# A fused multiply-add stream: y in two 64 KB loads, stores released by a semaphore after the third product

## The chip, the core and the metric

The kernel runs on one core of one Trainium2 chip. The metric is the device time of one execution in microseconds (us). Five runs of the kernel before are shown, and one further execution was taken with the hardware profiler. Sizes of "32 KB" and "64 KB" are bytes per partition; on 128 partitions they make transfers of 4 MB and 8 MB.

## The reference

```python
B, S, D = 1024, 16, 512      # bf16
def reference(x, y, gamma):  # x, y: [B, S, D], gamma: [D]
    return x + gamma * y
```

x, y and the result have 16,384 rows of 512 bf16 values, 16.78 MB each. So the kernel has to read 33.55 MB and write 16.78 MB, and for each element it does one product and one sum.

## The kernel before

Partition p holds the rows 128 p to 128 p + 127 of the flattened arrays, so each partition's part lies together in HBM. These 128 rows are cut into four pieces of 32 rows (`PIECES`), 32 KB per partition each. y has an SBUF buffer for all 128 rows and the results are written over it. x has a buffer of 64 rows, so that pieces 2 and 3 of x take the places of pieces 0 and 1.

**Queues.** SyncE (SP) issues all loads, in the order of the list `SP`, by `ring` (line 75 on): x 0, y 0, x 1, y 1, y 2, x 2, y 3, x 3, each of 4 MB (lines 88 and 91). ScalarE (ACT) issues gamma's load (line 85) and the four stores (line 95), by the list `ACT`. The two queues appear in the profile as q1 (SP) and q10 (ACT). The first x, the first y and gamma are moved to the head of the program (`EARLY`).

**Waits in the queues.** An engine executes its list in order, so a wait holds up everything behind it. A load of x that overwrites an old piece waits on the semaphore `s_add` for the add that has used the old piece: x 2 for add 0, x 3 for add 1 (`X_AFTER`). A store carries in its last number the add it waits for: stores 0, 1 and 2 all wait for add 2, store 3 for add 3.

**VectorE (DVE).** gamma is first spread over the 128 partitions: TensorE multiplies a row of ones with it into PSUM, and VectorE copies the result to SBUF (lines 104 to 110). Then, for each piece in turn, VectorE waits for the piece of y, multiplies it by gamma in place (line 115, "product"), waits for the piece of x and for the product, and adds (line 120, "add"). All eight instructions cover 128 x 16,384 elements.

**The end.** SP waits for the four adds and for all stores.

The lines that decide the order:

```python
X_AT = [0, 32, 0, 32]
X_AFTER = [-1, -1, 0, 1]
SP = [('x', 0), ('y', 0), ('x', 1), ('y', 1), ('y', 2), ('x', 2), ('y', 3), ('x', 3)]
ACT = [('g',), ('s', 0, 0, 2), ('s', 1, 1, 2), ('s', 2, 2, 2), ('s', 3, 3, 3)]
```

Of the kernel before, what the change touches and what calls it, by code (L numbers as in the profile page):

```python
# [3 lines left out]


PIECES = [32, 32, 32, 32]

X_AT = [0, 32, 0, 32]
X_AFTER = [-1, -1, 0, 1]


SP = [('x', 0), ('y', 0), ('x', 1), ('y', 1), ('y', 2), ('x', 2), ('y', 3), ('x', 3)]
ACT = [('g',), ('s', 0, 0, 2), ('s', 1, 1, 2), ('s', 2, 2, 2), ('s', 3, 3, 3)]

EARLY = [('x', 0), ('y', 0), ('g',)]
MULT, ADD = mybir.AluOpType.mult, mybir.AluOpType.add


def _take(sem, n, eng):


    return eng.wait_ge(sem, n).then_inc(sem, -n)  # L22


def kernel(
    tc: tile.TileContext,
    x: bass.AP,
    y: bass.AP,
    gamma: bass.AP,
    out: bass.AP,  # L30
):

    nc = tc.nc
    P = nc.NUM_PARTITIONS
    tc.close()
    tc.compile()  # L38

    xf = x.flatten_outer_dims()  # L40
    yf = y.flatten_outer_dims()
    of = out.flatten_outer_dims()
    N, D = xf.shape
    rows = N // P
    n = len(PIECES)
    assert sum(PIECES) == rows
    starts = [sum(PIECES[:c]) for c in range(n + 1)]
    dt = xf.dtype
    xv = xf.rearrange("(p n) d -> p n d", p=P)
    yv = yf.rearrange("(p n) d -> p n d", p=P)  # L50
    ov = of.rearrange("(p n) d -> p n d", p=P)

    gamma_row = nc.alloc_sbuf_tensor("gamma_row", [1, D], dt).ap()
    ones_row = nc.alloc_sbuf_tensor("ones_row", [1, P], dt).ap()
    gamma_sb = nc.alloc_sbuf_tensor("gamma_sb", [P, D], dt).ap()
    y_sb = nc.alloc_sbuf_tensor("y_sb", [P, rows, D], dt).ap()
    x_rows = max(a + r for a, r in zip(X_AT, PIECES))
    x_sb = nc.alloc_sbuf_tensor("x_sb", [P, x_rows, D], dt).ap()
    gamma_ps = nc.alloc_psum_tensor("gamma_ps", [P, D], mybir.dt.float32).ap()

    sem = nc.alloc_semaphore
    s_gamma, s_ones, s_ps, s_dve = sem("s_gamma"), sem("s_ones"), sem("s_ps"), sem("s_dve")
    s_x = [sem(f"s_x{c}") for c in range(n)]
    s_y = [sem(f"s_y{c}") for c in range(n)]
    s_add, s_end, s_out = sem("s_add"), sem("s_end"), sem("s_out")

    def piece(a, b=None):
        return slice(starts[a], starts[(a if b is None else b) + 1])

    def x_tile(c):  # L70
        return x_sb[:, X_AT[c] : X_AT[c] + PIECES[c], :]

    early, stores = [], 0

    def ring(eng, what, known=-1):

        nonlocal stores
        for w in what:
            kind, args = w[0], w[1:]
            need = X_AFTER[args[0]] if kind == "x" else args[2] if kind == "s" else -1  # L80
            if need > known:
                eng.wait_ge(s_add, need + 1)
                known = need
            if kind == "g":
                i = eng.dma_start(out=gamma_row, in_=gamma.unsqueeze(0)).then_inc(s_gamma, 16)
            elif kind == "x":
                c = args[0]
                i = eng.dma_start(out=x_tile(c), in_=xv[:, piece(c), :]).then_inc(s_x[c], 16)
            elif kind == "y":
                c = args[0]  # L90
                i = eng.dma_start(out=y_sb[:, piece(c), :], in_=yv[:, piece(c), :])
                i.then_inc(s_y[c], 16)
            else:
                r = piece(args[0], args[1])
                i = eng.dma_start(out=ov[:, r, :], in_=y_sb[:, r, :]).then_inc(s_out, 16)
                stores += 1
            if w in EARLY:
                early.append(i.ins)

    ring(nc.sync, SP)  # L100
    ring(nc.scalar, ACT)


    nc.vector.memset(ones_row, 1.0).then_inc(s_ones, 1)  # L104
    _take(s_ones, 1, nc.tensor)
    _take(s_gamma, 16, nc.tensor)
    nc.tensor.matmul(gamma_ps, ones_row, gamma_row, start=True, stop=True).then_inc(s_ps, 1)  # L107
    _take(s_ps, 1, nc.vector)
    nc.vector.tensor_copy(out=gamma_sb, in_=gamma_ps).then_inc(s_dve, 1)  # L109
    _take(s_dve, 1, nc.vector)  # L110

    for c in range(n):
        yt = y_sb[:, piece(c), :]
        _take(s_y[c], 16, nc.vector)
        nc.vector.tensor_tensor(  # L115
            out=yt, in0=yt, in1=gamma_sb[:, None, :].to_broadcast([P, PIECES[c], D]), op=MULT
        ).then_inc(s_dve, 1)
        _take(s_x[c], 16, nc.vector)
        _take(s_dve, 1, nc.vector)
        nc.vector.tensor_tensor(out=yt, in0=x_tile(c), in1=yt, op=ADD).then_inc(s_add, 1)  # L120


    nc.scalar.sem_inc(s_end, 1)
    _take(s_end, 1, nc.sync)
    _take(s_add, n, nc.sync)
    _take(s_out, 16 * stores, nc.sync)

    main = nc.main_func.blocks[0].instructions
    names = {i.name for i in early}
    for b in nc.main_func.blocks[1:]:  # L130
        for i in [i for i in b.instructions if i.name in names]:
            b.instructions.remove(i)
    for k, i in enumerate(early):
        main.insert(1 + k, i)


# [1 line left out]
_INS = ['x', 'y', 'gamma']  # L138
_OUTS = [((1024, 16, 512), 'bfloat16')]


# [23 lines left out]
```

## Time and profile before

| what | value |
|---|---|
| median of five runs | 120.96 us (120.2 to 121.08) |
| profiled execution, its own time | 120.48 us |
| its span, first to last instruction | 119.1 us |
| VectorE: four products | 34.8 us, 8689 ns each |
| VectorE: four adds | 34.8 us, 8692 ns each |
| VectorE idle before products | 17.6 us, of it 15.7 before the first |
| issue to landing, median: x / y / stores | 21.3 / 34.7 / 24.2 us |

The profile numbers the time from the first instruction. "Busy" of a compute engine is the time in which it executes; issuing a DMA isn't counted. The DMA rows give, for each queue, the number of packets, the megabytes and the share of sixteen DMA engines' span that these packets took. The time to landing of a transfer runs from its issue to its last completion, and so includes the time in which it stands behind earlier transfers of its queue.

### The profile page before, as it was taken

What the parts mean: (1) busy time and instruction counts of PE and PEld (TensorE: products, weight loads), DVE (VectorE), ACT (ScalarE), POOL (GpSimd) and SP (SyncE); (2) the same over time, 40 slices, a digit from 0 to 9 for tenths busy, and PEclk for the clock granted to TensorE, in tenths of its full rate; (3) what the DMA queues carried; (4) which work ended last, traced back from release to release, by engine and by line L of the source; (5) the groups of instructions that cost most, each with busy time, mean ns of one, the idle gap of its engine ahead of it and who ended that gap; (6) DMA issues with size and microseconds to landing.
All of it is one profiled execution on the core that took longest, in us unless ns stands there. A gap on an engine that the chain in (4) does not pass through costs nothing. (4 is left out here: it accounts for less than half of the span.)

```text
span 119.1 us, 84 instructions
## 1 busy us (share of the span) xinstructions
PE 0.6 (0%) x1; PEld 0.1 (0%) x1; DVE 70.2 (59%) x10; POOL 0.2 (0%) x4
## 2 busy tenths in 40 slices
PE   0100000000000000000000000000000000000000
PEld 0000000000000000000000000000000000000000
DVE  0100000699999399999999999999999400000000
POOL 0000000000000000000000000000000000000000
DMA  8989898989898998989898989989999898989895
GB/s 275 429 374 506 352 528 352 517 363 517 363 506 374 407 473 374 506 352 528 352 517 363 495 385 440 440 352 429 451 396 484 363 517 352 528 352 495 385 473 231
DMA packets 1730, 50.33 MB, mean 422 GB/s; under 512 B 193, under 2 KB 194, under 8 KB 194
## 3 DMA queue, kind: packets, MB, share of 16 engines
q1 hardware_dynamic: 1152, 33.55, 66.2%
q10 hardware_dynamic: 578, 16.78, 32.6%
HBM read 33.56 MB, written 16.78 MB: 422 GB/s over the span
## 5 line engine op out<-in xcount | busy, mean ns | idle before, releaser
L115 DVE TENSOR_TENSOR y_sb<-y_sb,gamma_sb 128x16384 bf16<-128x16384 bf16 x4 | 34.8, 8689 | 17.6 <-DVEq L22 17.6
L120 DVE TENSOR_TENSOR y_sb<-x_sb,y_sb 128x16384 bf16<-128x16384 bf16 x4 | 34.8, 8692 | 0.6
L109 DVE CAST gamma_sb<-gamma_ps 128x512 bf16<-128x512 f32 x1 | 0.7, 692 | 3.4 <-DVEq L22 3.4
L104 DVE MEMSET ones_row<- 1x128 bf16 x1 | 0.2, 165 | 2.0 <-PEq L38 2.0
L107 PE MATMUL gamma_ps<-gamma_row,ones_row 1*128 1x512 bf16 x1 | 0.6, 581 | 4.8 <-PEq L22 4.8
L107 PEld LDWEIGHTS gamma_ps<-gamma_row,ones_row 1*128 1x128 bf16 x1 | 0.1, 100 | 4.7 <-issue 4.7
L149 POOL MEMSET const-bfloat16-1.0<- 128x1 bf16 x1 | 0.1, 101 | 0.0
L149 POOL MEMSET const-uint8-127<- 128x1 uint8 x1 | 0.1, 101 | 0.0
L149 POOL MEMSET const-float32-0.0<- 128x1 f32 x1 | 0.1, 98 | 0.2 <-issue 0.2
L149 POOL MEMSET const-float32-1.0<- 128x1 f32 x1 | 0.1, 98 | 0.0
## 6 DMA issues: line engine op xcount, KB each, us to landing
x_sb<-in_x_dram SPq DMA_DIRECT2D x4, 4096.0 KB, 21.3
y_sb<-in_y_dram SPq DMA_DIRECT2D x4, 4096.0 KB, 34.7
out_dram<-y_sb ACTq DMA_DIRECT2D x4, 4096.0 KB, 24.2
gamma_row<-in_gamma_dram ACTq DMA_DIRECT2D x1, 1.0 KB
```

Of the source, the lines that this page charges most:

```text
L104: nc.vector.memset(ones_row, 1.0).then_inc(s_ones, 1)
L107: nc.tensor.matmul(gamma_ps, ones_row, gamma_row, start=True, stop=True).then_inc(s_ps, 1)
L109: nc.vector.tensor_copy(out=gamma_sb, in_=gamma_ps).then_inc(s_dve, 1)
L115: nc.vector.tensor_tensor(out=yt, in0=yt, in1=gamma_sb[:, None, :].to_broadcast([P, PIECES[c], D]), op=MULT).then_inc(s_dve, 1)
L120: nc.vector.tensor_tensor(out=yt, in0=x_tile(c), in1=yt, op=ADD).then_inc(s_add, 1)
L149: nc = _bacc.Bacc("TRN2", target_bir_lowering=False, num_devices=1)
```

## The change

The lists now name ranges of rows in place of numbers of pieces. The loads of x and the eight VectorE instructions stay in pieces of 32 rows; y is loaded in two transfers of 64 rows; the result is stored as 64, 32 and 32 rows. The order of the loads on SP is x 0-32, y 0-64, x 32-64, y 64-128, x 64-96, x 96-128. The last two wait for add 0 and add 1, as before. VectorE waits once for each load, at its first use.

A new semaphore `s_go` is increased by VectorE between product 2 and add 2, once product 2 is done. ACT waits for it ahead of its first store, and then for the adds of the rows that the store holds: add 1 for the first store, add 2 for the second, add 3 for the third. x 0-32, y 0-64 and gamma are at the head of the program.

```diff
-X_AT = [0, 32, 0, 32]
-X_AFTER = [-1, -1, 0, 1]
-SP = [('x', 0), ('y', 0), ('x', 1), ('y', 1), ('y', 2), ('x', 2), ('y', 3), ('x', 3)]
-ACT = [('g',), ('s', 0, 0, 2), ('s', 1, 1, 2), ('s', 2, 2, 2), ('s', 3, 3, 3)]
-EARLY = [('x', 0), ('y', 0), ('g',)]
+SP = [('x', 0, 32, 0), ('y', 0, 64), ('x', 32, 64, 32), ('y', 64, 128), ('x', 64, 96, 0), ('x', 96, 128, 32)]
+ACT = [('g',), ('s', 0, 64), ('s', 64, 96), ('s', 96, 128)]
+EARLY = (2, 1)
+DVE = [('m', 0), ('a', 0), ('m', 1), ('a', 1), ('m', 2), ('go',), ('a', 2), ('m', 3), ('a', 3)]
...
+    def frees(w):
+        old = x_loads[: x_loads.index(w)]
+        old = [v for v in old if meets(v[3], v[3] + v[2] - v[1], w[3], w[3] + w[2] - w[1])]
+        return [c for v in old for c in pieces_of(v[1], v[2])]
...
+            need = frees(w) if kind == "x" else pieces_of(w[1], w[2]) + list(w[3:]) if kind == "s" else []
+            need = max((order[c] + 1 for c in need), default=0)
+            if kind == "s" and not went and ("go",) in DVE:
+                _take(s_go, 1, eng)
+                went = True
             if need > known:
-                eng.wait_ge(s_add, need + 1)
+                eng.wait_ge(s_add, need)
                 known = need
...
-    for c in range(n):
-        yt = y_sb[:, piece(c), :]
-        _take(s_y[c], 16, nc.vector)
...
+    def need(loads, c):
+        for w in loads:
+            if w not in landed and meets(starts[c], starts[c + 1], w[1], w[2]):
+                _take(s_load[w], 16, nc.vector)
+                landed.add(w)
+    for kind, *args in DVE:
+        if kind == "go":
+            if open_mults:
+                _take(s_dve, open_mults, nc.vector)
+                open_mults = 0
+            nc.vector.sem_inc(s_go, 1)
+            continue
...
-    _take(s_out, 16 * stores, nc.sync)
+    _take(s_out, 16 * len(stores), nc.sync)
```

## The prediction

> **What bounds the kernel now.** I read the page's busy shares and DMA rows first, then the chain of waits, then the timeline of SP and of VectorE, and last the tiles with a narrow window around each issue, which gives the landing time of each transfer alone.
>
> ```profile
> span 119.1 us, 84 instructions
> PE 0.6 (0%) x1; PEld 0.1 (0%) x1; DVE 70.2 (59%) x10; POOL 0.2 (0%) x4
> DMA packets 1730, 50.33 MB, mean 422 GB/s; under 512 B 193, under 2 KB 194, under 8 KB 194
> q1 hardware_dynamic: 1152, 33.55, 66.2%
> q10 hardware_dynamic: 578, 16.78, 32.6%
> DVE 7%; issue 0%
> ```
>
> VectorE works 59% of the span. The packets of the two DMA queues fill 66.2% + 32.6% = 98.8% of what sixteen engines have. The chain of waits holds nothing but 7% of VectorE, since it breaks off at the last add: what ends last is a store, which this view does not follow. So the 16 DMA engines are the bound, and an edit counts only if it changes their work or leaves them idle.
>
> The packets: 1730 - 194 small ones = 1536 = 12 pieces x 128 partitions, so one packet is one partition's 32 KB row, and each engine moves 96. In q10, 0.326 x 16 x 119.1 us / 512 = 1.213 us a packet; the rounding of the share leaves 1.2115 to 1.215.
>
> ```profile
> 0.00 0.37 SPq L88 DMA_DIRECT2D x_sb<-in_x_dram  x1
> 0.42 0.42 SPq L91 DMA_DIRECT2D y_sb<-in_y_dram  x1
> 1.90 0.33 SPq L88 DMA_DIRECT2D x_sb<-in_x_dram  x1
> 2.28 0.92 SPq L91 DMA_DIRECT2D y_sb<-in_y_dram  x2
> 39.47 0.33 SPq L88 DMA_DIRECT2D x_sb<-in_x_dram  x1
> 39.84 0.44 SPq L91 DMA_DIRECT2D y_sb<-in_y_dram  x1
> 58.89 0.33 SPq L88 DMA_DIRECT2D x_sb<-in_x_dram  x1
> ```
>
> Each issue is start and duration. For single issues the tile view adds the time to landing: the first x, the last y, the last x, then the first and the last store.
>
> ```profile
> DMA to landing us min/median/max: 12.1/12.1/12.1
> ...
> DMA to landing us min/median/max: 30.5/30.5/30.5
> ...
> DMA to landing us min/median/max: 21.5/21.5/21.5
> ...
> DMA to landing us min/median/max: 13.7/13.7/13.7
> ...
> DMA to landing us min/median/max: 25.3/25.3/25.3
> ```
>
> Added to the issue times, the twelve 4 MB pieces land at 12.1, 21.7, 31.5, 41.2, 50.9, 60.7, 70.3, 80.4 (loads) and 90.0, 99.7, 109.5, 119.1 (stores). The step is 9.7 us = 8 packets x 1.213 everywhere but in two places: the first piece needs 12.1 (2.4 of start-up), and the last x needs 80.4 - 70.3 = 10.05, so some 0.35 us is lost while the stores, issued at 76.34, come in. The sum 12.1 + 11 x 9.7 + 0.35 = 119.15 is the span. Everything that can be won inside the span is therefore those 2.4 and 0.35 us and whatever part of 1.213 us isn't transfer.
>
> ```profile
> 21.91 8.69 DVE L115 TENSOR_TENSOR y_sb<-y_sb,gamma_sb 128x16384 bf16<-128x16384 bf16 x1 [15.71 <-DVEq L22]
> 30.75 8.69 DVE L120 TENSOR_TENSOR y_sb<-x_sb,y_sb 128x16384 bf16<-128x16384 bf16 x1
> 41.34 8.69 DVE L115 TENSOR_TENSOR y_sb<-y_sb,gamma_sb 128x16384 bf16<-128x16384 bf16 x1 [1.90 <-DVEq L22]
> 58.78 8.68 DVE L115 TENSOR_TENSOR y_sb<-y_sb,gamma_sb 128x16384 bf16<-128x16384 bf16 x1
> 76.22 8.69 DVE L115 TENSOR_TENSOR y_sb<-y_sb,gamma_sb 128x16384 bf16<-128x16384 bf16 x1
> 85.06 8.69 DVE L120 TENSOR_TENSOR y_sb<-x_sb,y_sb 128x16384 bf16<-128x16384 bf16 x1
> ```
>
> A product starts about 0.14 us after its y lands (41.2 to 41.34); product to add is 8.84 us (21.91 to 30.75), a pair 17.44 (41.34 to 58.78). VectorE ends at 93.75, and the last store's data are not moved before 109.5, so it has slack.
>
> **What the Trainium skill says.** "DMA: Bandwidth & Descriptors", section "Where 436 GB/s comes from", puts the ceiling at 435.2 GB/s over 16 engines. For 32,768 B on one engine that is 1.2047 us, an estimate from that page; the trace's 1.213 lies 8.6 ns above (7 to 10.5 with the rounding). The same page, "Queues, rings and completion order", says that an engine goes round-robin between the queue rows at packet boundaries; the trace, where the last x landed only 4.0 us after the first store was issued, shows at most little of such mixing. Its "Anatomy of one DMA" says that waits on semaphores happen on the issuing sequencer and DMA engines only consume their queues; the trace agrees, with SP's load issues held until the adds end (39.44 to 39.47). Its "Rules for kernel authors" want at least 1 MiB a transfer; all but gamma are 4 MB, and their step of 9.7 us is 432 GB/s, so nothing is left there.
>
> **The change part by part.**
>
> *Larger packets.* The bytes stay. y comes as two transfers of 128 rows of 64 KB, and so does the first store. Where a row stays one packet, 512 + 512 + 512 packets become 512 (x) + 256 (y) + 128 + 256 (stores) = 1152: 24 fewer on each engine. With 8.6 ns each (an estimate from the page's ceiling and the 1.213) that is 0.2 us; bounds 0 (the rows are cut again) and 0.25 (10.5 ns). I take -0.2. Three transfers fewer save three completions an engine; the step is 9.7 = 8 x 1.213 already, so nothing is seen of them: 0. Two SP issues (0.43 us each) and one ACT issue go, under running transfers: 0; uncovered they would cost as much again.
>
> *The order of the loads and VectorE's start.* Before, the first product needed the first 8 MB (21.7); now it needs x 0 and a y of 8 MB, 12 MB in all: the landing of the third piece, 31.5, less eight packets saved by then (0.07), so 31.4. Product 0 starts at 31.55, add 0 at 40.4, product 1 at 49.0, add 1 at 57.85, ending 66.55. Its x (41.2) has landed. Product 2 needs the second y: its landing is that of the sixth piece, 60.6, before its turn at 66.45. It ends at 75.15. Add 2 (x landed by 70.3) starts about 75.3, product 3 at 84.0, add 3 at 92.8, ending about 101.5. All waits on loads inside the chain are gone and VectorE ends 8 us later. That costs nothing, as the last store's data are due on the engines only at about 109.4; without this cover every microsecond would count in full.
>
> *SP's issue of the third and fourth x.* The buffers come free with adds 0 and 1. The third x goes out at 49.1 instead of 39.47, with the second y ahead of it until 60.6: covered by 11.5 us. The fourth goes out at 66.6 instead of 58.89. What is ahead ends at 70.2, so it is covered by 3.6 us where it had 11.4. Nothing but SP's end wait is queued behind it. To keep the line it must land by 70.2 + 9.7 = 79.9, which is 13.3 us after its issue. The trace has two issues onto an idle or new queue: the first x at 12.1 us to landing and the first store at 13.7 us. The second waited for the loads to drain, so it is an upper bound: with the first the x would be 1.2 us early, with the second 0.4 late. I take 0, and keep +0.4 and a restart for the slower side.
>
> *The release of the stores.* Before, ACT waited for add 2 (76.31); now it waits for an increment that VectorE makes after product 2, and then for add 1, long done. The issue moves from 76.34 to about 75.25. The added increment and ACT's second wait cost at most some 0.1 us of a VectorE that has 8 us to spare. Behind it on ACT are only the other stores: rows 64 to 96 wait for add 2 (84.0), rows 96 to 128 for add 3 (101.5). The first store of 8 MB keeps the engines busy from 80 to 99.4, the second to 109.1, so both arrive in time. The loads still have 4.6 us to run at the release, where they had 4.0. Stores thus meet about one load packet more. What the meeting costs is known only as 0.35 us in before; now it may be 0 (the first store is ready before the loads end) or 0.7 (each packet that meets pays again, and the store's packets are twice as long). I take the same 0.35: no change.
>
> **The sum.** -0.2 + 0 + 0 + 0: the span goes from 119.15 to 118.95, the profiled execution from 120.48 (1.4 outside the span, untouched) to 120.28. The median of the runs, 120.96, stands 0.48 above that execution; with the same offset I forecast 120.75. A measurement of this kernel can tell about 0.5% (0.6 us) from no change, so the forecast is "within 0.5%". Its own range is 120.4 to 121.2.
>
> **The rivals.**
>
> *Slower: SP's queue runs dry before the fourth x.* For it: the cover of its issue shrinks from 11.4 to 3.6 us. Against it: the first x of the kernel shows that 12.1 us to landing is possible, and 13.3 is enough. It decides from 13.3 us to landing on; the price is 0.4 us by the first store's figure and, on top, a restart, at most the first piece's excess over latency and transfer. The window up to 1.0 us moved almost nothing, so that excess is 12.1 - 1.0 - 9.7 = 1.4. Between 0.4 and 1.8 I take 1.0: 121.75.
>
> *Faster: the 0.35 us at the change from loads to stores goes as well.* For it: the store is issued earlier and has longer packets to fill with. Against it: the loss sits on the loads, which meet the stores for longer. 120.75 - 0.35 = 120.4, and with the packet saving at its upper end 120.35, on the 0.5% line; noise decides, mostly towards faster.
>
> *It does not do what it says:* a 64 KB row is cut into two packets again. Then the page's packet count stays near 1730, the saving is nothing, and the time 120.96.
>
> **How the numbers follow.** Forecast 0.45 (0.35 within, 0.05 to either side by noise); slower rival 0.23 (0.20 slower, 0.03 within); faster rival 0.22 (0.16 faster, 0.06 within); cut rows 0.10 (0.08 within, 0.01 each side). That gives faster 0.22, same 0.52, slower 0.26. The range runs from 120.1 (the faster rival with the scatter of the runs shown, 120.2 to 121.08) to 121.8 (the slower rival at its price); below and above lie about 1 in 10 each.
>
> **What would show it.** Packets: about 1300 (1152 large ones, 146 small), with q10 still near 32.5%. Product 0 starts at 31.5, add 3 ends at 101.5, and VectorE has no idle time in between. The fourth x lands at 79.9 to 83 (later where packets of the stores come between its own). The first store is issued at 75.25. A dip in the DMA row of the page near 70 us is the slower rival; a count near 1730 is the third. I am wrong altogether if a 64 KB packet takes much more than 2.42 us, or if reads beside writes cost more than 0.7 us.

## The result and the profile after

The changed kernel takes 120.89 us (median of 44 executions, 120.61 to 121.48), the kernel before 120.57 (79 executions). The ratio is 1.0033, 95% interval [1.0023, 1.0042]: 0.4 us slower. A second comparison, with new executions of both, gave the same 1.0033 [1.0018, 1.0049]. I had forecast 0.2 us faster, inside "within 0.5%". The time lies in the range and in that class, and the sign is wrong. That 120.89 lies so near the forecast 120.75 is luck: the forecast stood on five runs with a median of 120.96, and from the 120.57 of 79 executions the same saving would have led to 120.4. One experiment below (f2) has most of its executions over 1.5% above its fastest one, and the intervals count only those near the fastest, so its median is given beside its ratio.

From the page of the changed kernel:

```profile
span 119.4 us, 81 instructions
DMA  8999889988898989988998989998899888989894
DMA packets 1298, 50.33 MB, mean 421 GB/s; under 512 B 145, under 2 KB 146, under 8 KB 146
q1 hardware_dynamic: 864, 33.55, 66.2%
q10 hardware_dynamic: 434, 16.78, 32.5%
```

1298 - 146 = 1152 large packets, as forecast: each 64 KB row is one packet. The two shares sum to 98.7%, against 98.8% before, and the DMA row, 40 slices of the span in tenths, has no dip. So the engines were not left idle for longer; packets took longer than they needed.

From the timeline of the changed kernel (start, duration, what):

```profile
31.42 8.69 DVE L150 TENSOR_TENSOR y_sb<-y_sb,gamma_sb 128x16384 bf16<-128x16384 bf16 x1 [25.29 <-DVEq L23]
48.98 17.77 SPq L108 DMA_DIRECT2D x_sb<-in_x_dram  x2
66.31 8.69 DVE L150 TENSOR_TENSOR y_sb<-y_sb,gamma_sb 128x16384 bf16<-128x16384 bf16 x1
75.26 26.59 ACTq L114 DMA_DIRECT2D out_dram<-y_sb  x3
75.35 8.69 DVE L159 TENSOR_TENSOR y_sb<-x_sb,y_sb 128x16384 bf16<-128x16384 bf16 x1 [0.35 <-DVEq L23]
92.79 8.69 DVE L159 TENSOR_TENSOR y_sb<-x_sb,y_sb 128x16384 bf16<-128x16384 bf16 x1
```

VectorE does what was worked out: product 0 at 31.42 (forecast 31.55), release at 75.26 (75.25), last add ending at 101.48 (101.5), with one wait of 0.35 us on the way. So the loss is not there. The time to landing tells where it is. First the third and the fourth x, then the first and the last store, each from the tile view of its own window:

```profile
DMA to landing us min/median/max: 21.2/21.2/21.2
DMA to landing us min/median/max: 16.7/16.7/16.7
...
DMA to landing us min/median/max: 24.8/24.8/24.8
...
DMA to landing us min/median/max: 17.9/17.9/17.9
```

The third x lands at 48.98 + 21.2 = 70.2. Seven pieces of 4 MB are in by then; before, the seventh was in at 70.3, so the change leads by 0.1 there. With the first store ten pieces are done: 75.26 + 24.8 = 100.1 us. Before, the tenth was done at 99.7. The change lost half a microsecond between 70 and 100 us, and the last two pieces keep step (119.4 against 119.1). The fourth x lands at 66.42 + 16.7 = 83.1, where 79.9 would have been its turn. Most of this isn't lateness of its data. The window 82 to 83 us of the changed kernel:

```profile
q10 hardware_dynamic: 16, 1.05, 241.8%
q1 hardware_dynamic: 16, 0.00, 0.9%
```

No packet of either queue starts between 80.5 and 82 us. Then come the sixteen small packets that close the load, beside the second 64 KB packets of the store. So the closing packets stood behind one store packet of 2.4 us each, and without it the landing is 80.7, against 80.4 before.

A narrow window of the DMA view gives the mean length of a packet: share x 16 x width / number, where the number of 32 KB packets is the MB over 0.03277. A packet counts with its whole length where it starts, so a share can pass 100%. Here are the load queue's rows in the windows 68 to 71 us and 76 to 79 us, for the kernel before:

```profile
q1 hardware_dynamic: 63, 1.54, 119.4%
...
q1 hardware_dynamic: 32, 1.05, 94.8%
```

and for the changed kernel:

```profile
q1 hardware_dynamic: 57, 1.34, 110.7%
...
q1 hardware_dynamic: 35, 1.15, 107.9%
```

Before: 1.194 x 48 / 47 = 1.22 us in the first window (no loss against 1.213) and 0.948 x 48 / 32 = 1.42 in the second, about the 0.35 us that the prediction had read from the landings. After: 1.30 us in the first window and 1.48 in the second. So there are two places with stretched packets: near 69 us, 2 to 4 us after the fourth x was issued (66.42), and near 77 us, 1 to 3 us after the first store was issued (75.26).

### The profile page after: what moved, and what is told of

Same layout as the page of the kernel before. It is cut to its first block, busy times and chain, and to the rows that moved or that the text cites. A ratio compares the mean times of both kernels' runs of the same rounds, so it can differ in the third digit from the quotient of the medians.

```text
span 119.4 us, 81 instructions
## 1 busy us (share of the span) xinstructions
PE 0.6 (0%) x1; PEld 0.1 (0%) x1; DVE 70.1 (59%) x10; POOL 0.2 (0%) x4
## 2 busy tenths in 40 slices
DMA packets 1298, 50.33 MB, mean 421 GB/s; under 512 B 145, under 2 KB 146, under 8 KB 146
## 6 DMA issues: line engine op xcount, KB each, us to landing
out_dram<-y_sb ACTq DMA_DIRECT2D x1, 24.8
```

## The experiments

Three theories. **A**: the fourth x is issued with too little ahead of it (3.7 us of loads instead of 11.4). **C**: the stores are released too early, or (C1) their packets are too long at that point; C2 is the release time alone. **B**: 64 KB packets, or 32 KB ones behind them, are slower as such. Ratios are to the kernel before on the same chip, with 95% intervals. The diffs show the changed parts of lines, and "..." stands for lines left out.

| run | what it is | median us | ratio |
|---|---|---|---|
| e1 | changed, last x in two halves | 120.87 | 1.0042 [1.0025, 1.0059] |
| e2 | changed, 64 KB store as two | 121.03 | 1.0049 [1.0029, 1.0069] |
| e3 | before, 64 KB store | 120.33 | 0.9993 [0.9977, 1.0009] |
| e5 | changed, fourth x 1.3 us later | 121.01 | 1.0045 [1.0029, 1.0060] |
| f1 | changed, fourth x in time | 121.06 | 1.0052 [1.0034, 1.0071] |
| f2 | before, fourth x late (67.8) | 123.20 | 1.0005 [0.9982, 1.0028] |
| f3 | before, release 8.5 us earlier | 121.02 | 1.0057 [1.0039, 1.0076] |
| f4 | before, release 1.05 us earlier | 120.94 | 1.0049 [1.0032, 1.0067] |
| g1 | changed, release 1.1 us later | 120.75 | 1.0023 [1.0007, 1.0039] |
| g2 | changed, release 2.3 us later | 120.73 | 1.0018 [1.0005, 1.0031] |
| h1 | before, release 1.2 us later | 120.59 | 0.9994 [0.9971, 1.0018] |
| k1 | before, stores 64 and 64 KB | 120.25 | 0.9988 [0.9973, 1.0003] |
| m1 | changed, x in time, release later | 120.44 | 0.9995 [0.9974, 1.0016] |
| n1 | y 32, 32, 64; release at 76.6 | 120.28 | 0.9974 [0.9960, 0.9987] |
| n2 | n1, release at 75.6 | 120.79 | 1.0024 [1.0011, 1.0038] |
| p1 | before, fourth x late (66.8) | 120.67 | 1.0011 [0.9993, 1.0028] |
| q1 | k1, release 1.1 us later | 120.56 | 0.9989 [0.9973, 1.0006] |
| r1 | the changed kernel again | 120.93 | 1.0033 [1.0018, 1.0049] |

### The length of the packets (e2, e3, k1)

```diff
-ACT = [('g',), ('s', 0, 64), ('s', 64, 96), ('s', 96, 128)]
+ACT = [('g',), ('s', 0, 32), ('s', 32, 64), ('s', 64, 96), ('s', 96, 128)]    # e2
...
-('s', 0, 0, 2), ('s', 1, 1, 2), ('s', 2, 2, 2), ('s', 3, 3, 3)
+('s', 0, 1, 2), ('s', 2, 2, 2), ('s', 3, 3, 3)                                # e3
+('s', 0, 1, 2), ('s', 2, 3, 3)                                                # k1
```

> The changed kernel with its 64 KB store as two of 32 KB, same release. Theory C1 (the 64 KB store packets make the change from loads to stores dearer, 0.15 us): ratio to before falls from 1.0033 to about 1.0027 (0.15 won, 8 packets at 8 ns lost). Theory C2 (the length of the packet is nothing; the release, 1.1 us earlier, makes it dearer): ratio 1.0035 to 1.004.

> The kernel before with its first two stores as one of 64 KB, release unchanged (add 2). C1: 0.15 lost, 0.07 won, ratio 1.0005 to 1.001. C2: 0.07 won, ratio 0.9995. The landing of the last x stays at 80.4 if packets of stores don't come between its own.

> The kernel before with its four stores as two of 64 KB rows, the first released by add 2 and the second by add 3: 16 packets fewer an engine, of 8 ns each: 0.13 us, ratio 0.9989. If the first 64 KB store makes the meeting with the loads dearer: 1.000 to 1.001.

Long store packets are not the cause: without them the changed kernel is not faster (1.0049, with an interval above the 1.0027 that C1 expected), and put into the kernel before they don't measurably slow it. C1 falls by e2; the intervals of e3 and k1 alone would still reach into its figures. The two medians of e3 and k1 lie where a saving of 8 ns a packet puts them (0.9994 and 0.9989), but both intervals include 1, so the saving is bounded and not shown by them.

### The fourth x in halves, and a delayed fourth x (e1, f1, e5)

```diff
-PIECES = [32, 32, 32, 32]
+PIECES = [32, 16, 16, 32, 32]
...
-('x', 64, 96, 0), ('x', 96, 128, 32)]
+('x', 64, 96, 0), ('x', 96, 112, 32), ('x', 112, 128, 48)]
...
-        return [c for v in old for c in pieces_of(v[1], v[2])]
+        rows = [(v[1] + max(v[3], w[3]) - v[3], v[1] + min(v[2] - v[1], w[3] + w[2] - w[1] - v[3])) for v in old]
+        return [c for lo, hi in rows for c in pieces_of(lo, hi)]              # f1 alone
```

> The changed kernel, with product 1 and add 1 in two halves of 16 rows and the last x in two loads of 16 rows, each issued when its half of add 1 is done: the first half near 57.8 us instead of 66.4, the second at 66.4 with half a piece more ahead of it. Theory A (the fourth x is issued with only 3.7 us of loads ahead of it, and the engines lose some 0.25 us at that hand-over): the loss goes, 8 packets more per engine cost 0.07; the step from the landing of the second y to that of the third x falls from 9.83 to 9.70, ratio to before about 1.002. Rival B (the loss comes from 64 KB packets or from going back to 32 KB ones behind them): nothing is won, the step stays near 9.83, ratio 1.0035 to 1.004.

> As the run with the last x in halves, but the first half now really goes out after the first half of add 1 (near 57.9 us, 12 us of loads ahead of it) and the second at 66.9 with 8.5 us ahead. Theory A (late issue of the fourth x): the time falls against that run and the changed kernel, ratio to before 1.001 to 1.0025, least time near 120.3. Rival B (64 KB packets or the way back to 32 KB): 1.0035 to 1.0045, least time near 120.6.

> The changed kernel with four loads of gamma into spare rows issued ahead of the last x (behind the same wait), only to delay its issue by some 1.5 to 2 us; their data are 1 KB each. Theory A: the ahead of the queue shrinks from 3.7 to about 2 us and the loss grows by 0.3 to 1.5 us, ratio to before 1.006 to 1.016. Rival B: no more than the issue of small packets, ratio 1.003 to 1.0045.

e1 didn't do what it was to do: the wait was for all adds of the buffer's old load, so both halves went out at 67.0 us. f1 mends that (57.9 and 66.8), and the time did not fall. e5 issues four loads of 1 KB ahead of the fourth x, which went out only 1.3 us later (67.7), and theory A's 1.006 did not come; the small loads, though, put new work into the same queue at the old time. By these three runs A looked wrong. They share something else: all keep the release at 75.3 to 75.9 us.

### The release alone (f4, f3, h1)

```diff
+        if c == 2:
+            nc.vector.tensor_tensor(out=yt[:, :28, :], in0=x_tile(c)[:, :28, :], in1=yt[:, :28, :], op=ADD).then_inc(s_go, 1)
+            nc.vector.tensor_tensor(out=yt[:, 28:, :], in0=x_tile(c)[:, 28:, :], in1=yt[:, 28:, :], op=ADD).then_inc(s_add, 1)
...
+            if w[:2] == ("s", 0):
+                _take(s_go, 1, eng)
-('s', 0, 0, 2), ('s', 1, 1, 2)
+('s', 0, 0, 1), ('s', 1, 1, 1)                                                # f4
```

f3 has the increment after product 2 instead, with add 2 whole; h1 has it after 4 rows of product 3.

> The kernel before, with add 2 cut into 28 and 4 rows and the first two stores released by the first part, at 75.3 us as in the changed kernel instead of 76.3. C2 (release 1.1 us earlier is dearer): 0.15 to 0.3 us lost, ratio 1.0015 to 1.0025. Otherwise 1.000.

> The release part of the change alone: the kernel before, its first store released by a semaphore that VectorE increases after product 2, here at 67.6 us instead of 76.3, with 12.5 us of loads still to run. Store 2 waits for add 2, store 3 for add 3. The fourth x lands between 85 and 91 as the queues take turns. If every packet of a load that meets a store pays: some 10 packets an engine instead of two, 1.0 us or more lost, ratio 1.008. If only the first meeting pays, whatever its time: 1.000 (0.0005 either way). If stores and loads together fill the engines better: 0.997.

> The kernel before with product 3 cut into 4 and 28 rows and the first three stores released by its first part, at 77.4 us instead of 76.3. C2 alone: 0.998 to 1.000 (its 0.35 us at the meeting may go). A store that needs 3.2 us to its first packet: 0.6 us idle, 1.004 to 1.005.

This is the finding. In the kernel before, with every packet and load as it was, a release at 75.3 us instead of 76.3 costs 0.49%, 0.6 us, more than the whole change. f4's load queue in the window 76 to 79 us, and the landing of its fourth x, issued at 58.82:

```profile
q1 hardware_dynamic: 29, 0.95, 101.7%
```

```profile
DMA to landing us min/median/max: 23.2/23.2/23.2
```

1.017 x 48 / 29 = 1.68 us a packet, against 1.42 before, and the fourth x lands at 82.0 instead of 80.4; all but 0.4 us of that is again one store packet (1.2 us) ahead of its closing packets. The work is the same; each packet in that stretch takes longer. It is not a price for every packet that loads and stores run side by side. f3 releases 8.5 us earlier (67.87), and the loss is no larger (0.57%, intervals overlapping). Its load queue in the window 68 to 71 us, and both queues in 76 to 80 us:

```profile
q1 hardware_dynamic: 54, 1.25, 115.6%
...
q1 hardware_dynamic: 29, 0.95, 55.0%
q10 hardware_dynamic: 24, 0.79, 45.5%
```

The stretch follows the release: 1.156 x 48 / 38 = 1.46 us at 68 to 71, and 1.21 us for loads and stores alike once they take turns (0.550 x 64 / 29, 0.455 x 64 / 24). Going later than 76.3 gains nothing clear (h1).

### The release in the changed kernel (g1, g2)

```diff
-('m', 2), ('go',), ('a', 2)
+('m', 2), ('a', 2)
...
+            if c == 2:
+                nc.vector.tensor_tensor(out=yt[:, :3, :], in0=xt[:, :3, :], in1=yt[:, :3, :], op=ADD).then_inc(s_go, 1)
+                xt, yt = xt[:, 3:, :], yt[:, 3:, :]                            # g1; g2 with 8
```

> The changed kernel with the release moved from the end of product 2 (75.26) to the end of the first 3 rows of add 2, which is cut into 3 and 29 rows: near 76.2 us, 3.5 us before the loads would end, about as in the kernel before. C2 (an earlier release is what costs): the loss goes and the packet saving shows, ratio 0.997 to 1.000. Theory A (late fourth x) or B (64 KB packets): 1.003 as before.

> The same with 8 and 24 rows: release near 77.6 us, 2.1 us before the loads would end. If the store's first packets need 2 us or less from its issue: as the run with 3 rows, or better (0.996 to 1.000). If they need 3.2 us, which is what the kernel before shows at most: 1 us of idle engines, ratio 1.005 to 1.008.

C2 alone expected 1.000 or less, and that did not come: only 0.1% was won, with overlapping intervals. The two windows of g1 (68 to 71, 76 to 79):

```profile
q1 hardware_dynamic: 58, 1.38, 115.9%
...
q1 hardware_dynamic: 36, 1.18, 95.5%
```

The second window has come down to 0.955 x 48 / 36 = 1.27 us. The first stands at 1.159 x 48 / 42 = 1.32. So in this execution, with the release mended, the stretch behind the fourth x's issue is what is left.

### Both mended, and the late x alone (m1, n1, p1)

```diff
-('y', 0, 64), ('x', 32, 64, 32), ('y', 64, 128)
+('y', 0, 32), ('x', 32, 64, 32), ('y', 32, 64), ('y', 64, 128)                 # n1
...
+                nc.vector.tensor_tensor(out=yt[:, :22, :], in0=xt[:, :22, :], in1=yt[:, :22, :], op=ADD).then_inc(s_go, 1)    # n1
...
+            nc.vector.tensor_tensor(out=yt[:, :28, :], in0=yt[:, :28, :], in1=g[:, :28, :], op=MULT).then_inc(s_late, 1)
...
+            if w == ("x", 3):
+                _take(s_late, 1, eng)                                          # p1
```

m1 is f1 with the release after 2 rows of add 2 (76.4 us).

> The changed kernel with both suspects taken away: the last x in two halves that go out at 57.9 and 66.8 us, and the release moved to about 76.2 us (after 2 rows of add 2). If both the late issue of the fourth x (A) and the early release (C2) cost: the packet saving of 0.13 us is left, ratio 0.998 to 1.000. If A is nothing and 64 KB loads of y cost (B): 1.002, as with the release moved alone.

> The changed kernel with the first half of y in two loads of 32 KB, so that VectorE starts at 21.9 us and the fourth x goes out at 58.9; the second half of y and the first store stay at 64 KB; release after 22 rows of add 2, near 76.4 us. A and C2: both losses gone, 16 packets fewer than before: ratio 0.998 to 1.000. B: 1.001 to 1.002.

> The kernel before with product 2 cut into 28 and 4 rows and the fourth x issued after its first part, at 66.5 us, as in the changed kernel (3.7 us of loads ahead of it instead of 11.4). Nothing else moves. A: 0.2 to 0.3 us lost, ratio 1.0015 to 1.003, and the step from the landing of y 3 to that of the fourth x grows. B: 1.000 (0.0005 either way).

With the fourth x in time and the release at 76.4 to 76.6 us the loss is gone (m1), and n1, with the second half of y and the first store at 64 KB, is 0.26% faster than before, clear of 1. m1 differs from f1 in the release alone, 76.43 against 75.64 us, and their intervals don't meet (0.9995 and 1.0052). That ends B: m1 has all the long packets of the changed kernel, and n1 has some of both kinds. The windows of n1:

```profile
q1 hardware_dynamic: 64, 1.57, 121.9%
...
q1 hardware_dynamic: 32, 1.05, 84.9%
```

1.22 and 1.27 us: no stretch behind the fourth x (issued at 58.81), and little at the meeting.

The late fourth x by itself, in the kernel before (p1), gives 1.0011 with an interval that includes 1, and its first window shows no stretch (1.22 us). p1's loads were running 0.7 us late when it was issued, so it had 4.3 us ahead of it rather than 3.7. What A costs alone in the kernel before therefore stays open, between nothing and 0.3%. In the changed kernel with a late release it does cost: g1 and g2, with the late fourth x, have 1.0023 and 1.0018, and n1, with the fourth x in time, 0.9974, with intervals that don't meet. n1 also has the first half of y in two loads; m1, which doesn't, has 0.9995, and its interval meets theirs. So this cost is some 0.2 to 0.5%, less sure than that of the release.

> The kernel before, with the fourth x issued after product 2 (67.6 us) in place of add 1 (58.9), so that 2.8 us of loads are ahead of it where the changed kernel has 3.7. All packets are 32 KB and the stores are as before. Theory A: 0.25 to 0.6 us are lost, ratio 1.002 to 1.005. Rival B, and a theory in which all of the loss is from the stores' release: 1.000.

f2 (fourth x at 67.8) took 120.23 to 120.65 us in four of its 14 executions and 123.03 to 123.65 in ten; no execution of any other kernel here took more than 122.00. Whether the still later issue makes the ten long was not tested, so I draw nothing from it.

### The release once more, and the changed kernel again (n2, r1)

n2 is n1 with 18 rows in place of 22.

> The fastest version so far (second half of y and first store at 64 KB, fourth x issued at 58.9) with one thing changed: release after 18 rows of add 2 instead of 22, near 75.4 us instead of 76.5. C2 (an earlier release alone costs): 0.3 to 0.5 us lost against that version, ratio to before 1.000 to 1.002. If the release costs only beside a late fourth x: 0.9975.

> The changed kernel as it is, once more beside the run before it on the same chip: ratio 1.0025 to 1.004; in its profile stretched packets near 69 us (late fourth x) and near 77 us (release).

n1 and n2 differ in one number, the release at 76.58 or 75.57 us, and their ratios are 0.9974 and 1.0024 with intervals that don't meet. n2's second window, and the landing of its fourth x (issued at 58.86):

```profile
q1 hardware_dynamic: 31, 1.02, 103.2%
```

```profile
DMA to landing us min/median/max: 24.2/24.2/24.2
```

1.60 us a packet where n1 has 1.27, and a landing at 83.1 where n1 has 58.81 + 21.4 = 80.2. The windows of r1, the changed kernel's second profile:

```profile
q1 hardware_dynamic: 56, 1.31, 108.5%
...
q1 hardware_dynamic: 35, 1.15, 103.4%
```

1.30 and 1.42 us: the stretch near 69 us comes again at the same size, (1.30 - 1.22) x 40 / 16 = 0.2 us an engine. e2, g1 and g2, which issue the fourth x as late, have it too (1.37, 1.32 and 1.28 us); e5, where it went out still later, doesn't (1.22). The one near 77 is within what single executions scatter, and that is much: k1, released at 76.36 like the kernel before, has 0.835 x 48 / 32 = 1.25 us in the second window, where that has 1.42, and e5, released at 75.30, has 1.087 x 48 / 40 = 1.30, in an execution of 120.50 us, the fastest of its 22. So a window shows where the time went in one execution; it is the ratios that carry the argument.

### The best version (q1)

> The kernel before with its stores as two of 64 KB and the first released at 77.4 us (after 4 rows of product 3) in place of 76.3: the packet saving of 0.13 us and up to 0.35 us of the meeting: ratio 0.996 to 0.999.

q1 (two 64 KB stores, release at 77.4) does not differ from k1: the later release adds nothing to it. n1 stays the only version clear of the kernel before.

## Why the prediction was wrong

**The bound and the packet count** were right: 1298 packets, DMA engines 98.7% filled, VectorE's times all within 0.15 us.

**Larger packets, -0.2 us.** No run measures this alone in time. The packets do: the window 82 to 83 us above has 2.418 us for 64 KB, 8 ns less than 2 x 1.213, and 24 x 8 ns = 0.19 us. e3 and k1 fit this, without being clear of 1.

**The release of the stores** is the step that failed. It said that a release 1.1 us earlier makes the stores meet about one load packet more, kept 0 to 0.7 us for the meeting, and took "the same 0.35: no change". Measured by itself it adds 0.6 us: 0.49% in the kernel before (f4), 0.50% between n1 and n2, 0.57% between m1 and f1. The place was right and the term was mis-sized. The 0.35 us of the kernel before, read from one execution, was taken as the fixed price of a change from loads to stores. The runs show a price that depends on when the stores are released.

**SP's issue of the fourth x**, taken at 0 and kept as the slower rival at 1.0 us, is the second step that failed, by less. Both profiles of the changed kernel show 0.2 us of stretched packets behind that issue, but not the dry queue that the rival described: the DMA row doesn't dip. In the changed kernel itself, mending it alone didn't help (f1), and mending the release alone won little (g1, g2). Only both together took the loss away (m1, n1). The two losses so do not add up, and why one hides behind the other was not found.

**The sum** was -0.2. With the release at its measured size it is -0.2 + 0.6 = +0.4 us, and the measured ratio is 0.0033 x 120.57 = 0.4 us. This agreement proves little: it leaves the fourth x at 0, and g1, with the release mended in the changed kernel itself, won only 0.1%. What is shown is that the loss needs both steps mended to go. The faster rival, that the 0.35 us would go as well, comes nearest in n1, released at 76.6 instead of 75.3 and with the fourth x in time; its 0.26% is 0.3 us, of which 16 packets fewer explain 0.13.

## What to carry to other kernels

When the DMA engines are full, look for stretched packets rather than for idle time: the mean packet length in a window of 3 us behind each issue shows a loss that busy shares hide. Where a second queue takes over from a first, set its issue by the end of the first one's last transfer, and try a microsecond either way; here, with loads due to end near 80 us, a release at 76.6 us was good and one at 75.6 was 0.5% dearer (n1, n2). A signal that seems to be an equal of an old one (the third product in place of the third add) is a new release time, and has to be priced as that.

## What was not expected of the hardware

In the profiles of f3, f4 and n2, issuing a store while several packets an engine of loads were outstanding stretched those packets from 1.21 to 1.46, 1.68 and 1.60 us on average over 3 us, once. In f3 both queues then took turns at 1.21 us a packet, and its 8.5 us of lead cost no more than one (1.0057, and 1.0049 in f4). Which part of the DMA engine loses this time was not seen. A row of 64 KB went as one packet, in loads and in stores.
